# Row stores issued one at a time in the next block's gate steps, and a weight piece's bound and scale moved up by a step

## The chip, the cores and the metric

One core of one Trainium2 chip runs the whole program. The metric is the device time of one execution in microseconds (us). Three runs of the kernel before gave 1183.08 to 1185.95 us, with a median of 1185.08 us.

## The reference, cut to what matters

The program is an attention between tokens and states, a gated MLP and a mixture of experts with one expert per token, one after the other:

```
attention   B=8, H=8, S=512 tokens, 32 states, D=64:
            xread = softmax(x state^T) state;  sread = softmax(state x^T) x
            x = concat([xread, sread])  -> 8 * 544 = 4352 rows of 512
MLP         x = (sigmoid(x @ w_gate) * (x @ w_val)) @ w_out     512 -> 1536 -> 512
experts     logits = x @ g;  e = argmax(logits);  p = softmax(logits)[e]
            out[row] = p * (relu(x[row] @ w1[e]) @ w2[e])       8 experts, 512 -> 1024 -> 512
```

The MLP's weights come as 64-bit floats; the expert weights w1 and w2 as 32-bit floats.

## The kernel before, in words

Every large product is made of three 16-bit products: each operand is split into a high and a low half (`pair`, lines 313 to 322: ScalarE writes the high half, L321 or L318, and VectorE or GpSimd the low one, L322 or L319).

`token_block(b)` runs eight times, once for each of the B = 8 sequences. It has 12 gate steps (`gate_val`, one for each 128 columns of w_gate and w_val) and then 4 output steps (`mlp_out`, one for each 128 tokens). A gate step is 12 matmuls of 512 columns, six into each of two PSUM tiles (L682 to L684); there are four such tiles (`mm`), so TensorE can work on one gate step while the one before it is being read. Behind the matmuls stand, in this order, a sigmoid on ScalarE (L688, writes `g`), a product on VectorE (L690, `g` in place), a cast on ScalarE (L695, `acth`) and a subtraction on GpSimd (L696, `actl`). `g` has two buffers: the sigmoid of a gate step can't start before the subtraction of the gate step two back has read its buffer.

Between pieces of a block's own matmuls stand numbered slots. `mid()` counts them: two in each gate step (slots 1 to 24: one behind the gate's matmuls, one behind the subtraction) and three in each output step (slots 25 to 36). In a slot, `mid()` first runs the functions that were hung on that number with `at(slot, f)`: the next block's attention, the state's scale, and the routing. Then it takes one step (up to the next `yield`) of a background generator with `pump(bg)`, in the gate steps in two slots of three, in the output steps in each. In blocks 1 to 7 that generator is `conv_experts`: it converts 64 pieces (128x1024 elements) of the expert weights into high and low halves. Each piece takes three steps. Its parts: `load` (a transfer on SyncE's queue, L628), `bound` (ScalarE sums absolute values, L634, into `em`), `scale` (TensorE spreads `em` over the partitions, L202; VectorE takes the maximum, L209, and makes a power of two, L142 and L143, `inv`), `pair` with that scale (L321 and L322), and a store of the two halves to DRAM on GpSimd's queue (L667, `w_d`). The store of a piece is issued in the next piece's second step.

`route(q, ...)` makes the routing of block q's 512 tokens in four steps, in slots 27, 29, 34 and 36 of the same block (for q = 0 in slots 35 and 36 of block 0 and 3 and 6 of block 1). Its last step writes the weight and the number of each token into the row (L838, L839) and issues four indirect DMAs on GpSimd's queue (L842), one for each 128 rows, which put the rows where their expert will read them (`rows_d`). All write the same tensor, so each one waits for the landing of the one before it. `xrow` has four buffers, written again in the next block's output steps.

Behind the eight blocks, the 256 state rows take 12 gate steps of their own (with `hook(fc)` behind each), and then some 37 expert tiles follow, which read `rows_d` and the converted weights.

The order of TensorE's instructions is that of the program, written by hand. On the other engines a planner orders each engine's queue beforehand; each queue then runs strictly in order. In blocks 1 to 7, what a slot issues is pinned behind the last sigmoid and the last product issued so far (`behind`).

Of the kernel before, what the change touches and what calls it, by code (L numbers as in the profile page):

```python
# [26 lines left out]
def attention_moe_router_kernel(  # L27
# [25 lines left out]
    B, H, S, D = x.shape  # L53
# [79 lines left out]
    def tl(shape, dt=F32, name="t", bufs=None, pool=None):  # L133
        kw = {} if bufs is None else {"bufs": bufs}
        return (pool or tiny).tile(shape, dt, name=name, tag=name, **kw)
# [177 lines left out]
    def pair(v, h16, l16, s=None, inplace=False):  # L313

        if inplace:
            nc.scalar.activation(v, v, AF.Copy, scale=s)
        if s is None or inplace:
            nc.scalar.copy(h16, v)  # L318
            nc.gpsimd.tensor_tensor(l16, v, h16, op=ALU.subtract)  # L319
        else:  # L320
            nc.scalar.activation(h16, v, AF.Copy, scale=s)  # L321
            nc.vector.scalar_tensor_tensor(l16, v, s, h16, op0=ALU.mult, op1=ALU.subtract)  # L322
# [288 lines left out]
    def conv_experts():  # L611

        items = [(e, i, k) for e in range(NE) for i in range(NFQ) for k in range(2)]
        vs = {}
        sc = {}

        def load(n):
            if n >= len(items):
                return
            e, i, k = items[n]  # L620
            q = slice(i * FQ, (i + 1) * FQ)
            if k == 0:
                vs[n] = big_p.tile([P, NDC, FQ], F32, name="big", tag="big")
                src = w1[e, :, q].rearrange("(c p) f -> p c f", p=P)
            else:
                vs[n] = big_p.tile([P, FQ // P, DM], F32, name="big", tag="big")
                src = w2[e, q, :].rearrange("(g p) w -> p g w", p=P)
            nc.sync.dma_start(out=vs[n], in_=src)  # L628

        def bound(n):  # L630
            if n >= len(items):
                return
            sc[n] = tl([P, 1], name="em")
            nc.scalar.activation(junk8, vs[n].rearrange("p a f -> p (a f)"), AF.Abs,  # L634
                                 accum_out=sc[n], saturate=False)

        def scale(n):
            if n >= len(items):
                return
            e, i, k = items[n]  # L640
            sc[n], _ = pow2_scale(
                all_max(spread(sc[n]), "er"), 14, "es", inv=False,
                out=inv12[:, k, e, i:i + 1],
            )

        for n in range(3):
            load(n)
        yield
        yield
        bound(0)  # L650
        yield
        scale(0)
        yield
        late = None
        for n, (e, i, k) in enumerate(items):
            v = vs.pop(n)
            if k == 0:
                o = big_p.tile([P, NDC, 2, FQ], F16, name="out", tag="out", bufs=2)
                dst = w1_d[e, :, i]
            else:  # L660
                o = big_p.tile([P, FQ // P, 2, DM], F16, name="out", tag="out", bufs=2)
                dst = w2_d[e, :, 2 * i:2 * i + 2]
            pair(v, o[:, :, 0], o[:, :, 1], sc.pop(n))
            yield
            bound(n + 1)
            if late:
                nc.gpsimd.dma_start(out=late[0], in_=late[1])  # L667
            late = dst, o
            yield
            load(n + 3)  # L670
            scale(n + 1)
            yield
        nc.gpsimd.dma_start(out=late[0], in_=late[1])

# [81 lines left out]
    def route(q, n, acts):  # L756
# [3 lines left out]
        for a in range(NFC // 4):  # L760
            for l in range(2):
                for i in range(4):
                    fc = 4 * a + i
# [71 lines left out]
        for j in range(n):  # L835
# [11 lines left out]
                bounds_check=NROWS - 1,  # L847
                oob_is_err=False,
            )
        yield  # L850

    def counts(nm):

# [238 lines left out]
    UMAX = (((22, 23), (34, 36)), ((6, 8), (20, 22)), ((6, 8), (20, 22)))  # L1092
    EARLY = 34
    ROUTE = (27, 29, 34, 36)
    GV, ALL = 2 * NFC, 2 * NFC + 3 * NJ

    sr = {}
    gens = {}
    router = {}
# [16 lines left out]
    def token_block(b):  # L1116
        isig = states[b]["i"]
        acts = []
        sg = tl([P, NFC], name="sgf")
        todo = {}  # L1120

        def at(slot, f):
            todo.setdefault(slot, []).append(f)

        if b + 1 < B:
            if b == 0:
                for u, slots in ((state_max(1), (13, 15)), (unit_max(NU), (14, 16))):
                    for slot in slots:
                        at(slot, lambda u=u: next(u, None))
            at(2 if b else 19, lambda: state_turn(b + 1))  # L1130

            def first_step(n):
                gens[n] = att_unit(n)
                next(gens[n])

            for c in range(NU):
                n = NU * (b + 1) + c
                slots = (UNIT0, UNIT1)[b][c] if b < 2 else UNIT[c]
                if slots[0]:
                    at(slots[0], lambda n=n: first_step(n))  # L1140
                for slot in slots[1:]:
                    at(slot, lambda n=n: next(gens[n], None))
                if LOAD[min(b, 2)][c]:
                    at(LOAD[min(b, 2)][c], lambda n=n: unit_load(n + 1))
                um = unit_max(n + 1)
                for slot in UMAX[min(b, 2)][c]:
                    at(slot, lambda um=um: next(um, None))
            if 1 <= b < B - 2:
                at(EARLY, lambda: first_step(NU * (b + 2)))
                at(EARLY + 2, lambda: unit_load(NU * (b + 2) + 1))  # L1150
            for m in range(NFP):
                at(GV + 2 * m, lambda m=m: drain(deque([state_weights(b + 1, m)])))
        if b + 1 == B:
            rs = state_rows()
            at(6, lambda: next(rs, None))
            at(12, lambda: next(rs, None))
        if b + 2 < B:
            at(1 if b else 21, lambda: state_load(b + 2))
            sm = state_max(b + 2)
            at(9 if b else 30, lambda: next(sm, None))  # L1160
            at(12 if b else 33, lambda: next(sm, None))
        if b == 0:

            rw = router_weights()
            for slot in (25, 26, 27, 28, 29, 30, 31, 33):
                at(slot, lambda: next(rw, None))
        for slot in (35, 36) if b == 0 else ROUTE:
            at(slot, lambda: next(router[b], None))
        if b == 1:
            for slot in (3, 6):  # L1170
                at(slot, lambda: next(router[0], None))
        half = [0]

        def mid():
            half[0] += 1
            with behind() if b else ExitStack():
                for f in todo.get(half[0], ()):
                    f()
                if half[0] > 12 if b == 0 else half[0] > GV or half[0] % 3:
                    pump(bg)  # L1180

        if b > 0:
            nc.vector.tensor_scalar(
                sg, inv_w[:, 0], isig, 2.0 ** (M_SH - PR_SH), ALU.mult, ALU.mult
            )
        for fc in range(NFC):
            if b == 0 and fc % 2 == 0:
                fp = fc // 2
                if fp == 0:
                    ws = state_weights(0, 0)  # L1190
                    drain(deque([ws]))
                nc.vector.tensor_scalar(
                    sg[:, fc:fc + 2], inv_w[:, 0, fc:fc + 2], isig, 2.0 ** (M_SH - PR_SH),
                    ALU.mult, ALU.mult,
                )
                if fp + 2 < NFP:
                    cvs[fp + 2] = conv_wgv(fp + 2, raws.pop(fp + 2))
                    next(cvs[fp + 2])
                    if fp + 3 < NFP:
                        raws[fp + 3] = load_wgv(fp + 3)  # L1200
            elif b == 0 and fc // 2 + 2 < NFP:
                drain(deque([cvs.pop(fc // 2 + 2)]))
            gate_val(fc, S, sg, V_SH, token_chunks(b, fc), acts, mid)
            if b == 0 and fc + 2 < NFC:
                if fc % 2 == 0:
                    ws = state_weights(0, fc // 2 + 1)
                next(ws, None)
        if b == 0:
            drain(bg)
        rt_new(b, isig)  # L1210
        router[b] = route(b, NJ, acts)
        for j in range(NJ):
            mlp_out(NJ * b + j, j, acts, mid)
        if b == 0:
            bg.append(ce)
# [84 lines left out]
    n = B * NS  # L1300

    def hook(fc):

        if fc == 4:
            prelim()
            fetch_w(0, regs["e"], which=(0,))
        if fc == 8:
            fetch_w(0, regs["e"], which=(1,))
            for s in range(2):
                fetch_rows(s, regs["row"] + s * P)  # L1310
# [184 lines left out]
```

## Time and profile before

| what | value |
|---|---|
| runs of the kernel before | 1183.08, 1185.08, 1185.95 us |
| the profiled execution's own time | 1188.41 us |
| its span, first to last instruction | 1186.4 us |
| mean granted TensorE clock | 0.963 |
| busy in the span: TensorE matmuls, VectorE, ScalarE, GpSimd | 91%, 72%, 47%, 24% |
| indirect stores of rows (L842) | 34, mean 1162 ns of GpSimd each |
| pieces converted | 64 |

PE is TensorE, PEld its weight load, DVE VectorE, ACT ScalarE, POOL GpSimd, SP SyncE. "X <- Y" after an idle time says that the instruction waited for Y. The shares are averages over stages with different limits: blocks 1 to 7 lie between about 198 and 744 us, the state rows between 744 and 777 us, the expert tiles behind that.

### The profile page before, as it was taken

The page shows a single profiled execution, that of the slowest core. Times are in us where ns is not written, and L with a number is a line of the kernel's source. Part 1 is how long each engine was busy: PE and PEld are TensorE (multiplying, and loading weights), DVE is VectorE, ACT ScalarE, POOL GpSimd, SP SyncE. Part 2 cuts the span into 40 slices and gives each one's busy share as a digit, 9 for nine tenths or more (in the row PEclk, how much of TensorE's full clock was granted, in tenths as well). Part 3 has the DMA queues.
Part 4 walks back from the last instruction along what each step waited for, and adds up shares of the span by engine and source line. Part 5 has one row for each costly group of instructions (what it writes and reads, how often), then busy time and mean ns, then how long its engine had stood idle before and what let it go on. Part 6 is the DMA issues. An engine that isn't in the chain of part 4 may idle for free. (4 is left out here: it accounts for less than half of the span.)

```text
span 1186.4 us, 22619 instructions
## 1 busy us (share of the span) xinstructions
PE 1083.8 (91%) x8459; PEld 592.4 (50%) x8459; DVE 852.7 (72%) x2080; ACT 554.4 (47%) x967; POOL 284.8 (24%) x293
## 2 busy tenths in 40 slices
PE   3377489899899999998999999999999999999997
PEld 2222134344344444443444444856666667766675
DVE  7999775687888888978878765348666666665664
ACT  4666644676766858767668582311111111111111
POOL 1112200532524506324145171300100000000000
PEclk9678799999999999999999999999999999999999
DMA  7615492556647577466575452563321495979438
GB/s 257 199 56 160 107 173 57 154 145 192 203 134 222 166 179 228 142 170 201 137 232 152 143 205 77 156 223 128 74 55 39 116 364 116 319 255 379 71 81 298
DMA packets 187745, 200.66 MB, mean 169 GB/s; under 512 B 130159, under 2 KB 154735, under 8 KB 184304
## 3 DMA queue, kind: packets, MB, share of 16 engines
q1 hardware_dynamic: 172736, 147.51, 44.7%
q0 software_dynamic: 14896, 51.67, 11.5%
q8 instruction: 68, 1.11, 0.4%
q14 instruction: 45, 0.37, 0.1%
HBM read 217.40 MB, written 54.88 MB: 230 GB/s over the span
## 5 line engine op out<-in xcount | busy, mean ns | idle before, releaser
L930 ACT CAST acth<-v 128x256 f16<-128x256 f32 x148 | 59.9, 404 | 329.2 <-DVE v L929 299.1
L696 POOL TENSOR_TENSOR actl<-g,acth 128x512 f16<-128x512 f32 (+1 forms) x108 | 138.6, 1286 | 197.7 <-ACT acth L695 197.2
L684 PE MATMUL mm<-aT,M 128*128 128x512 f16 x384 | 152.5, 397 | 13.8 <-ACT M L510 13.8
L682 PE MATMUL mm<-aT,M 128*128 128x512 f16 x384 | 152.2, 396 | 14.0 <-ACT g L688 13.3
L739 PE MATMUL mm<-wout,acth 128*128 128x512 f16 x408 | 155.6, 381 | 9.5 <-DVE wout L607 8.5
L740 PE MATMUL mm<-wout,acth 128*128 128x512 f16 x408 | 155.4, 381 | 0.0
L741 PE MATMUL mm<-wout,actl 128*128 128x512 f16 x408 | 155.3, 381 | 0.0
L683 PE MATMUL mm<-aT,M 128*128 128x512 f16 x384 | 151.9, 395 | 0.0
L915 PEld LDWEIGHTS <-wgv 128*128 128x128 f16 x1184 | 115.8, 98 | 18.5 <-DMA wgv<-w_d 1.2
L915 PE MATMUL mm<-big,wgv 128*128 128x256 f16 x704 | 118.5, 273 | 0.7 <-DMA wgv<-w_d 0.7
L944 POOL DMA_INDIRECT out_dram<-g,meta x37 | 36.0, 972 | 344.4 <-DVE g L941 284.7
L918 PEld LDWEIGHTS <-wgv 128*128 128x128 f16 x1184 | 115.8, 98 | 4.0
L918 PE MATMUL mm<-big,wgv 128*128 128x128 f16 x704 | 117.3, 219 | 0.0
L928 DVE TENSOR_REDUCE v<-mm 128x256 f32<-128x512 f32 x148 | 101.4, 685 | 18.6 <-PE mm L918 18.6
L931 DVE TENSOR_TENSOR actl<-v,acth 128x256 f16<-128x256 f32 x148 | 62.8, 424 | 68.8 <-ACT acth L930 67.8
L322 DVE SCALAR_TENSOR_TENSOR out<-big,inv,out 128x1024 f16<-128x1024 f32 x64 | 82.9, 1295 | 36.3 <-ACT out L321 36.3
L690 DVE SCALAR_TENSOR_TENSOR g<-mm,g 128x512 f32<-128x512 f32 (+1 forms) x108 | 71.0, 657 | 50.7 <-PE mm L684 26.0
L321 ACT ACTIVATE out<-big,inv 128x1024 f16<-128x1024 f32 x64 | 73.2, 1144 | 52.6 <-DVE inv L143 45.5
L688 ACT ACTIVATE g<-mm,sgf 128x512 f32<-128x512 f32 (+1 forms) x108 | 71.4, 661 | 41.2 <-POOL actl L696 30.8
L695 ACT CAST acth<-g 128x512 f16<-128x512 f32 (+1 forms) x108 | 63.3, 588 | 41.2 <-DVE g L690 41.0
L667 POOL DMA_DIRECT2D w_d<-out x63 | 35.5, 563 | 189.3 <-DVE out L322 138.1
L915 PE MATMUL mm<-out,wgv 128*128 128x256 f16 x480 | 80.8, 273 | 0.0
(322 smaller groups left out, 2126.7 us busy)
## 6 DMA issues: line engine op xcount, KB each, us to landing
wgv<-w_d SPq DMA_DIRECT2D x56, 2048.0 KB
wout<-w_d SPq DMA_DIRECT2D x18, 2048.0 KB
big<-in_moe_w_dram SPq DMA_DIRECT2D x64, 512.0 KB
w_d<-out POOLq DMA_DIRECT2D x64, 512.0 KB, 5.1
xb<-in_x_dram SPq DMA_DIRECT2D x60, 128.0 KB
wgv<-in_moe_w_gate_dram SPq DMA_DIRECT2D x3, 1024.0 KB
wgv<-in_moe_w_val_dram SPq DMA_DIRECT2D x3, 1024.0 KB
wout<-in_moe_w_gate_dram SPq DMA_DIRECT2D x3, 1024.0 KB
```

The lines of the kernel that those rows point to most:

```text
L321: nc.scalar.activation(h16, v, AF.Copy, scale=s)
L322: nc.vector.scalar_tensor_tensor(l16, v, s, h16, op0=ALU.mult, op1=ALU.subtract)
L682: nc.tensor.matmul(ps[k], w[0], v[0], start=(i == 0), stop=False)
L683: nc.tensor.matmul(ps[k], w[0], v[1], start=False, stop=False)
L684: nc.tensor.matmul(ps[k], w[1], v[0], start=False, stop=(i == len(parts) - 1))
L696: last["P"] = nc.gpsimd.tensor_tensor(lo, g, h, op=ALU.subtract)
L739: nc.tensor.matmul(po, hj, wout[:, fc, 1], start=(fc == 0), stop=False)
L740: nc.tensor.matmul(po, hj, wout[:, fc, 0], start=False, stop=False)
L741: nc.tensor.matmul(po, lj, wout[:, fc, 1], start=False, stop=(fc == NFC - 1))
L915: nc.tensor.matmul(ph[:, i], w1s[:, pr, c, 0, f], t[:, :, c], start=(c == 0), stop=False)
L918: nc.tensor.matmul(ph[:, i, 1], w1s[:, pr, c, 1, f], t[:, 0, c], start=False, stop=(c == NDC - 1),)
L928: nc.vector.tensor_reduce(v, ph.rearrange("p i l q -> p i q l"), axis=AX.X, op=ALU.add)
```

## The change

The store of a row group ends a step of `route`, so its last step becomes four. The first of them stays in slot 36 (block 0: slot 6 of block 1); the other three go to slots 3, 7 and 11 of the next block (10, 14 and 18 in block 1), and for the last block to the first three `hook` calls of the state rows. Only the two copies into the row and the indirect DMA of a group move; the arithmetic ahead of them stays in the first of the four steps.

In `conv_experts`, `bound(n + 1)` is issued ahead of `pair` of piece n in its first step, no longer in its second; `scale(n + 1)` in the second step, no longer in the third. `load(n + 3)` and the store stay where they were, and a piece still has three steps.

```
 conv_experts:
+            bound(n + 1)
             pair(v, o[:, :, 0], o[:, :, 1], sc.pop(n))
             yield
-            bound(n + 1)
+            scale(n + 1)
             if late:
                 nc.gpsimd.dma_start(out=late[0], in_=late[1])
             late = dst, o
             yield
             load(n + 3)
-            scale(n + 1)
             yield
 route, behind the indirect DMA of row group j:
                 oob_is_err=False,
             )
-        yield
+            yield
 constants:
     ROUTE = (27, 29, 34, 36)
+    ROWS = ((10, 14, 18), (3, 7, 11))
 token_block(b):
+        if b > 0:
+            for slot in ROWS[b > 1]:
+                at(slot, lambda: next(router[b - 1], None))
 hook(fc):
+        if fc < 3:
+            next(router[B - 1], None)
```

## Rows read from the trace of the kernel before

**Rows 1.** Blocks 1, 2, 4, state rows: PE PEld DVE ACT POOL busy, PEclk.
```profile
198.00:286.00 88.00, 80.46 (x576) 35.56 (x575) 67.86 (x200) 58.24 (x95) 28.30 (x27) 0.96 0.52 146
286.00:369.00 83.00, 79.54 (x582) 35.34 (x581) 67.87 (x175) 58.85 (x95) 29.14 (x29) 0.98 0.61 181
...
445.00:521.00 76.00, 74.01 (x556) 33.31 (x553) 64.74 (x160) 53.26 (x89) 29.68 (x28) 1.00 0.62 178
744.00:777.00 33.00, 33.00 (x287) 27.79 (x285) 8.79 (x40) 10.65 (x25) 12.79 (x18) 1.00 0.59 199
```

**Rows 2.** Waits of TensorE between 198 and 720 us: total, times, longest.
```profile
PE mm L682 <- ACT g L688: 9.4, 5, 3.4
PE at L202 <- ACT junk L634: 4.6, 5, 1.4
PE at L807 <- DVE roh L800: 2.3, 1, 2.3
```

**Rows 3.** Waits of the other engines in the same stretch.
```profile
ACT g L688 <- POOL actl L696: 30.8, 21, 3.9
POOL rows_d L842 <- DMA rows_d<-xrow,rri: 28.6, 15, 3.6
```

**Rows 4.** Timeline of block 1: start, duration, engine and line, idle before.
```profile
228.70 1.03 POOL L842 DMA_INDIRECT rows_d<-xrow,rri  x1 [2.99 <-DMA rows_d<-xrow,rri]
229.73 1.19 POOL L696 TENSOR_TENSOR actl<-g,acth 128x512 f16<-128x512 f32 x1
...
230.96 0.69 ACT L688 ACTIVATE g<-mm,sgf 128x512 f32<-128x512 f32 x1 [3.91 <-POOL actl L696]
...
231.69 0.38 PE L682 MATMUL mm<-aT,M 128*128 128x512 f16 x1 [3.44 <-ACT g L688]
...
231.91 0.38 PE L683 MATMUL mm<-aT,M 128*128 128x512 f16 x1
```

**Rows 5.** Behind a wait of block 1, of block 2; columns as above.
```profile
231.70:235.50 3.80, 3.80 (x11) 1.36 (x11) 1.80 (x5) 3.05 (x6) 2.23 (x2) 0.56 0.33 138
307.20:310.60 3.40, 3.40 (x9) 1.21 (x8) 3.40 (x7) 1.01 (x2) 0.74 (x2) 0.51 0.27 78
```

**Rows 6.** Timeline of block 2 around 303 us.
```profile
303.52 0.99 POOL L842 DMA_INDIRECT rows_d<-xrow,rri  x1 [3.60 <-DMA rows_d<-xrow,rri]
...
303.78 4.66 DVE L337 SCALAR_TENSOR_TENSOR xn<-xb,uxs,xn 128x256 f16<-128x256 f32 x4 [1.55 <-issue]
...
305.09 2.27 POOL L696 TENSOR_TENSOR actl<-g,acth 128x512 f16<-128x512 f32 x2
...
307.03 0.41 PE L682 MATMUL mm<-aT,M 128*128 128x512 f16 x1 [2.06 <-ACT g L688]
```

**Rows 7.** The four instructions of line 337 in that stretch: min/median/max ns.
```profile
L337 DVE SCALAR_TENSOR_TENSOR xn<-xb,uxs,xn x4: 472/478/3471, 303.8 to 308.0; 128x256 f16<-128x256 f32 x4
```

**Rows 8.** Line 842 in the whole span: min/median/max on GpSimd, and to landing.
```profile
L842 POOL DMA_INDIRECT rows_d<-xrow,rri x34: 974/1021/2232, 212.5 to 801.6; - x34
...
DMA to landing us min/median/max: 2.8/3.6/6.7
```

**Rows 9.** Groups of instructions by line: busy us, mean ns, idle before.
```profile
L321 ACT ACTIVATE out<-big,inv 128x1024 f16<-128x1024 f32 x64 | 73.2, 1144 | 52.6 <-DVE inv L143 45.5 <-DVE cum L817 7.0
...
L634 ACT ACTIVATE junk<-big 128x1024 fp8e5<-128x1024 f32 x64 | 67.3, 1052 | 0.0
...
L634 ACT ACTIVATION_READ_ACCUMULATOR junk<-big 128x1 f32 x64 | 12.5, 196 | 0.0
```

**Rows 10.** Timeline of block 2: a spread that waits for its bound.
```profile
314.17 0.23 PE L202 MATMUL at<-identb,em 128*128 128x128 bf16 x1 [1.40 <-ACT junk L634]
```

**Rows 11.** ScalarE in block 6: a sigmoid that waits.
```profile
620.83 0.69 ACT L688 ACTIVATE g<-mm,sgf 128x512 f32<-128x512 f32 x1 [3.53 <-POOL actl L696]
```

**Rows 12.** Busy time in a stretch of block 6 and one of block 3.
```profile
620.00:630.00 10.00, 10.00 (x51) 4.21 (x49) 4.60 (x9) 8.31 (x14) 5.48 (x6) 1.00 0.62 173
370.00:400.00 30.00, 28.84 (x154) 12.95 (x153) 22.89 (x62) 24.54 (x41) 18.74 (x17) 1.00 0.73 236
```

More of the change, by code (lines that the diff above doesn't have):

```diff
@@ L662, in conv_experts @@
                 dst = w2_d[e, :, 2 * i:2 * i + 2]
+            bound(n + 1)
             pair(v, o[:, :, 0], o[:, :, 1], sc.pop(n))
             yield
-            bound(n + 1)
+            scale(n + 1)
             if late:
@@ L670, in conv_experts @@
             load(n + 3)
-            scale(n + 1)
             yield
@@ L849, in route @@
             )
-        yield
+            yield
     def counts(nm):
@@ L1094, in attention_moe_router_kernel @@
     ROUTE = (27, 29, 34, 36)
+    ROWS = ((10, 14, 18), (3, 7, 11))
     GV, ALL = 2 * NFC, 2 * NFC + 3 * NJ
@@ L1171, in token_block @@
                 at(slot, lambda: next(router[0], None))
+        if b > 0:
+            for slot in ROWS[b > 1]:
+                at(slot, lambda: next(router[b - 1], None))
         half = [0]
@@ L1302, in hook @@
     def hook(fc):
+        if fc < 3:
+            next(router[B - 1], None)
         if fc == 4:
```

## Prediction, made before the result was known

> **What bounds the kernel now.** I read the busy time by stretch first. From the blocks on, TensorE's matmuls fill nearly all of the time: the state rows are full to the last tenth, block 4 has 74 us of work in 76 us, and so have blocks 3, 6 and 7 or nearly. Blocks 1 and 2, and 5, which repeats 2, stand out, with 88 and 83 us and a granted clock under 1.00 [rows 1]. So time can be won only where TensorE waits or runs slowly, and the waits are few. Between 198 and 720 us they are: 9.4 us in five waits for a sigmoid (L682 <- L688), 4.6 us in five waits of the spread for a bound (L202 <- L634), and 2.3 us for the routing in block 1 [rows 2]; all others are under 1.3 us in sum.
>
> Next I asked what the sigmoid waited for. On ScalarE it stood 30.8 us, 21 times, for the subtraction that frees a `g` buffer, and GpSimd, whose subtraction it is, stood 28.6 us, 15 times, in a row store that waits for the landing of the one before [rows 3]. The timeline of block 1 shows one such chain whole: the store waits 2.99 us, the subtraction queued behind it starts at 229.73 us, the sigmoid at 230.96, the matmul at 231.69 after 3.44 us of idling [rows 4]. In the 3.8 us behind it the granted clock was 0.56 of the full level, nearly all of it at 1.2 in place of 2.4 GHz; behind the like wait of block 2 it was 0.51 over 3.4 us, and the same in block 5 [rows 5]. A wait for a store thus costs its own length and then half of some 3.5 us.
>
> Blocks 2 and 5 have one link more. There the fourth store waited 3.60 us; then two subtractions ran back to back for 2.27 us, and TensorE idled for 2.06 us [rows 6]; block 5 has the same chain. Beside them, one of four equal VectorE instructions took 3471 ns, where the median is 478 [rows 7].
>
> **The change part by part.**
>
> *The stores.* No store is taken away: 34 before and after, 1.02 us of GpSimd each, 3.6 us to landing, 6.7 at most [rows 8]. What moves is when each is queued. Before, all four are issued in one slot, and the planner lays them between the subtractions of the first gate steps, where the next one comes up before the last has landed. After, they come four slots apart. A gate step is 12 matmuls, 0.22 us apart [rows 4], so 2.6 us, and four slots are two of them, 5.2 us. A store and its landing take 1.0 + 3.6 = 4.6 us: the median one no longer waits. The longest (1.0 + 6.7 = 7.7 us) still would, for 2.5 us. Behind a store on GpSimd stand the subtraction and then a piece's store to DRAM; for the subtraction waits the sigmoid two gate steps on, and for that the matmuls.
>
> What this frees: the five waits, 9.4 us [rows 2], and the slow stretches behind three of them. From the clock rows: 3.8 x (1 - 0.56) + 2 x 3.4 x (1 - 0.51) = 1.7 + 3.3 = 5.0 us [rows 5]. Bounds: nothing, if another wait takes their place, and 14.4 us. I take all of it here, and put what comes back into a term of its own.
>
> *The two copies into the row* move with each store; they are single elements on VectorE, which is busy for 22.89 of 30 us in the gate steps [rows 12]. Nothing is added to their number; I take 0.
>
> *The last block's stores* come one gate step of the state rows apart: 33 us for 12 steps, 2.75 us [rows 1], under the 4.6 us that a store needs, so they go on waiting, by some 1.9 us each. TensorE is busy for 33.00 of 33.00 us there now [rows 1], with the same four stores in the same stretch; that work hides them. Without this cover it would be 3 x 1.9 = 5.7 us. I take 0. The first read of the rows is issued five gate steps behind the last store, 13.7 us, which is more than the longest landing.
>
> *Bound and scale.* A bound is 1052 + 196 ns of ScalarE, the high half 1144 ns [rows 9]. Before, they stood in two steps, high half first; after, both in the first step, bound first. The spread keeps its distance of one step from the bound. Where that is one slot, 1.3 us, it is about the bound's own length, and TensorE waits whenever ScalarE is behind: in block 2 the spread at 314.17 us came after 1.40 us of it [rows 10]. Gain: the bound no longer stands behind a high half that itself waits for the scale (45.5 us of waiting before L321 [rows 9], most of it in output steps, where it costs nothing). Bounds: all 4.6 us of the spread's waits [rows 2] on one side; on the other, as much again, because the rotation of three steps over the slots is the same and the waits may only move. Nearest is the row of block 2, where ScalarE had just come out of the store's backlog: I take 1 us of gain. The load has to be there a step earlier; before, no bound ever waited (idle 0.0 [rows 9]), so I take 0, and at most one output slot of 2.6 us at a time.
>
> *What comes back.* In the gate steps ScalarE is busy for 24.54 of 30 us [rows 12]; with GpSimd free, it is the next to be late. Bound and high half in one slot are 2.4 us of it, where before at most 1.25 us came at once. A sigmoid of block 6, however, started 3.53 us late [rows 11], and TensorE was busy for 10.00 of the 10.00 us around it [rows 12]. So a delay of this size by itself is taken up by the four PSUM tiles; only delays that meet reach TensorE. Bounds: 0, and 1.25 us for each of the 37 pieces that fall into gate steps (64 x 16 of 28 steps), 46 us. Near the lower end: I take 3 us for this and for stores that still wait.
>
> *Sum.* -9.4 - 5.0 - 1 + 3 = -12.4 us. The profiled execution took 1188.4 us, so 1176.0; it stands 3.3 us above the median of the runs, which makes **1173 us**.
>
> **The rivals.**
>
> *Half of it.* In blocks 2 and 5 the late part is also VectorE's: 3471 against 478 ns is 3.0 us [rows 7], and it ends with the two subtractions, not with the store. If those two waits come about without the stores, only 9.4 - 2 x 2.06 = 5.3 us and one slow stretch of 1.7 us go, less the 2 us that come back on balance: -5 us, **1180 us**. For it: the change removes no subtraction. Against it: they were back to back because a store had held them. The Trainium skill ("SBUF — State Buffer", Who interferes with whom) has a rule on this side: a VectorE instruction with two SBUF inputs and a GpSimd instruction that reads SBUF exclude each other, for the whole instruction. By that rule these meetings stay possible wherever the stores stand, and the time would be that of this rival; the long instruction of line 337 fits it.
>
> *More.* The spread's waits go too and little comes back: -9.4 - 5.0 - 4.6 + 1 = -18 us, **1167 us**. For it: the longest of the five, 1.40 us, is the one just behind the backlog of block 2 [rows 10], and block 5 has its like. Against it: the other three stand elsewhere.
>
> *No change that can be told.* ScalarE is the next limit at once, and each sigmoid is late behind a bound and a high half where it was late behind a store: the five waits shrink by a third, 3 us, the slow stretches stay, and 1 us comes back: **1183 us**. For it: 24.54 of 30 us [rows 12]. Against it: the 3.53 us that cost nothing [rows 11, 12].
>
> *Slower.* The pair of 2.4 us in one slot ahead of a sigmoid. If 0.6 us of it reached TensorE for each of 37 pieces, that is 22 us against 14.4 won: +8 us, **1193 us**. It decides from 14.4 / 37 = 0.39 us for each piece. For it: ScalarE's 82% in such a stretch [rows 12]. Against it: a longer delay of one sigmoid, 3.53 us, was taken up whole [rows 11, 12].
>
> **How the numbers follow.** Forecast 0.58 (its own range 1168 to 1178), half 0.11, more 0.09, no change 0.13, slower 0.09. A measurement of this kernel can tell about 0.3% (3.6 us) from no change: the first three are faster, 0.78; same 0.13; slower 0.09. The range goes down just past the case of more, 1165, and up to 1183, past the half and to the time of no change, which leaves out some 0.18: the slower case, half of no change, and the tail under 1165.
>
> **What would show it.** Right: GpSimd's waits of line 842 for a landing fall from 28.6 us to under 10, ScalarE's waits for GpSimd from 30.8 to under 15; TensorE's five waits for the sigmoid are gone or under 2 us in sum; blocks 2 and 5 last some 77 us at a clock of 1.00; block 1 keeps the 2.3 us for the routing. Wrong: the stores no longer wait, and TensorE still idles at L682 (no change), or waits at L202 and L682 appear that are short, many, and spread over all blocks (slower); or line 337 still has an instruction of 3 us in blocks 2 and 5 (half).

## The result, and the profile after

The changed kernel took 1193.57 us (median of 6 runs, 1191.26 to 1197.49) beside 1185.51 us for the kernel before (6 runs, 1183.08 to 1186.8). The ratio is 1.0068, 95% interval [1.0042, 1.0094]: 8 us slower, where 12 us of gain were forecast. The profiled execution of the changed kernel took 1192.08 us, 3.7 more than that of the kernel before; it lies 1.5 us under its median, as the one of before lies 3.3 above.

The page's first part, then the instructions of line 842 with their landing:

```profile
span 1190.4 us, 22630 instructions
...
PE 1079.2 (91%) x8459; PEld 592.3 (50%) x8459; DVE 856.9 (72%) x2080; ACT 554.5 (47%) x967; POOL 275.4 (23%) x293
```

```profile
L842 POOL DMA_INDIRECT rows_d<-xrow,rri x34: 978/1019/1432, 210.1 to 805.7; - x34
...
  DMA rows_d<-xrow,rri: 5.1, 4
...
DMA to landing us min/median/max: 2.8/3.5/5.1
```

The stores did what was expected. In the blocks they hardly wait for each other's landing any more: 28.6 us in 15 waits before, between 198 and 720 us [rows 3], and 1.4 us in one wait after. The other three of the four waits shown (3.8 us) lie in the state rows. The waits of TensorE between 198 and 720 us, then one of ScalarE (total, times, longest), show what that was worth:

```profile
PE at L365 <- DMA xT<-xn: 16.6, 5, 8.1
PE at L202 <- ACT junk L634: 3.5, 3, 1.9
PE at L807 <- DVE roh L800: 2.3, 1, 2.3
...
PE mm L682 <- ACT g L688: 0.3, 1, 0.3
```

```profile
ACT g L688 <- POOL actl L696: 21.9, 22, 2.6
```

The wait for the sigmoid fell from 9.4 to 0.3 us [rows 2]. A wait that was no row of the argument took its place: 16.6 us at L365, the scores of the next sequence's attention, for `xT`, which SyncE's transposing DMA (L344) makes out of `xn`. Before, it was 0.5 us.

By blocks (distance from the first gate matmul of one block to that of the next, from the timeline), blocks 1 to 7 took 86.5, 80.3, 77.2, 77.5, 80.2, 75.5 and 66.2 us before, and 85.0, 78.7, 78.2, 87.3, 77.0, 76.3 and 66.2 after. Blocks 1, 2 and 5 won 6.3 us; block 4, where nothing was to be won, lost 9.8. The state rows took 48.2 us both times. Blocks 1, 2, 4 and part of the state rows in the columns of [rows 1] (DMA share and GB/s at the end):

```profile
198.00:283.00 85.00, 77.09 (x568) 34.06 (x567) 67.17 (x198) 60.04 (x96) 27.27 (x27) 0.98 0.60 159
283.00:361.70 78.70, 76.67 (x562) 34.24 (x561) 64.57 (x169) 54.67 (x91) 27.86 (x28) 0.98 0.61 177
439.90:527.20 87.30, 77.36 (x563) 34.23 (x562) 65.27 (x172) 57.12 (x94) 27.90 (x28) 0.94 0.62 168
...
748.00:781.00 33.00, 33.00 (x290) 28.06 (x288) 9.30 (x41) 11.24 (x25) 12.76 (x18) 1.00 0.58 191
```

Block 4 now has 77.36 us of TensorE in 87.3 us, at a clock of 0.94. Before, the same block was nearly full, at 1.00:

```profile
442.10:519.60 77.50, 75.51 (x568) 33.96 (x565) 66.24 (x169) 54.63 (x90) 29.68 (x28) 1.00 0.63 180
```

The place in block 4 where the time is lost, after, from four engines' queues (an SPq row starts when the DMA is issued; line 333 makes the high half of `xn`; a piece's store is line 667 before and 668 after):

```profile
457.45 1.14 ACT L333 ACTIVATE xn<-xb,uxs 128x1024 f16<-128x1024 f32 x1
462.56 1.78 SPq L285 DMA_DIRECT2D xb<-in_x_dram  x4
464.38 3.40 SPq L344 DMA_TRANSPOSE xT<-xn  x1
464.85 0.59 POOL L668 DMA_DIRECT2D w_d<-out  x1 [3.43 <-DVE sgs L143]
467.88 2.28 SPq L628 DMA_DIRECT2D big<-in_moe_w_dram  x2
474.85 1.49 PE L365 MATMUL at<-xT,bdT 128*64 128x512 f16 x6 [8.13 <-DMA xT<-xn]
```

and the same place before:

```profile
456.11 1.15 ACT L333 ACTIVATE xn<-xb,uxs 128x1024 f16<-128x1024 f32 x1
462.35 1.78 SPq L285 DMA_DIRECT2D xb<-in_x_dram  x4
464.17 2.98 SPq L344 DMA_TRANSPOSE xT<-xn  x1
465.96 0.58 POOL L667 DMA_DIRECT2D w_d<-out  x1
467.25 9.91 SPq L628 DMA_DIRECT2D big<-in_moe_w_dram  x3
469.88 0.84 PE L365 MATMUL at<-xT,bdT 128*64 128x512 f16 x6 [0.48 <-DMA xT<-xn]
```

The transpose is issued at nearly the same time, 464.2 and 464.4 us, with the same four x loads just ahead of it and a piece's load 3.1 and 3.5 us behind it. Before, its reader started 5.7 us later; after, 10.5 us later. A piece's store of 512 KB came 1.79 us behind the transpose before, and 0.47 us after. Measured from the block's first gate matmul (442.1 us before, 439.2 after), TensorE was ready for L365 at the same point, 27.3 and 27.5 us; but the transpose was issued 22.1 us into the block before and 25.2 after, since the high half of `xn` began at 14.0 and 18.2 us. So to the 0.5 us of before, two parts were added: 3 us of a later issue and 4.8 us of a slower transfer. Two-microsecond windows over the stretch (columns as above) show the DMA engines in it, after:

```profile
466.00:468.00 2.00, 0.72 (x4) 0.10 (x2) 1.97 (x5) 1.44 (x2) 1.85 (x2) 1.00 1.23 129
468.00:470.00 2.00, 0.00 (x0) 0.00 (x0) 1.93 (x4) 2.00 (x4) 0.67 (x1) 0.85 1.42 126
470.00:472.00 2.00, 0.00 (x0) 0.00 (x0) 0.35 (x1) 0.42 (x2) 0.57 (x1) 0.50 1.19 113
...
476.30:479.80 3.50, 3.50 (x11) 1.25 (x10) 0.68 (x2) 2.14 (x4) 0.00 (x0) 0.52 0.39 156
```

and before:

```profile
466.00:468.00 2.00, 2.00 (x11) 0.94 (x10) 1.97 (x7) 1.71 (x3) 1.54 (x3) 1.00 1.25 227
468.00:470.00 2.00, 1.52 (x9) 0.55 (x9) 0.98 (x2) 2.00 (x5) 0.15 (x1) 1.00 0.87 248
```

They are at least as busy as before and move half as much: 113 to 129 GB/s, not 227 to 248. The last row of after is the second price of an idle TensorE: 3.5 us at a clock of 0.52 behind the wait. The Trainium skill ("DMA: Bandwidth & Descriptors", Issuing engines are not separate DMA queues) says that transfers issued from different engines run on the same 16 DMA engines and interleave. The trace fits that: the transpose stands on SyncE's queue and the store on GpSimd's, and the one took 10.5 us with the other close behind. Whether the one slows the other is put to the test below (store_short).

### The profile page after: what moved, and what is told of

The parts are those of the page before. It is cut to its first block, busy times and chain, and to the rows that moved or that the text cites. A ratio compares the mean times of both kernels' runs of the same rounds, so it can differ in the third digit from the quotient of the medians.

```text
span 1190.4 us, 22630 instructions
## 1 busy us (share of the span) xinstructions
PE 1079.2 (91%) x8459; PEld 592.3 (50%) x8459; DVE 856.9 (72%) x2080; ACT 554.5 (47%) x967; POOL 275.4 (23%) x293
## 5 line engine op out<-in xcount | busy, mean ns | idle before, releaser
L696 POOL TENSOR_TENSOR actl<-g,acth 128x512 f16<-128x512 f32 (+1 forms) x108 | 133.8, 1243 | 189.3 <-ACT acth L695 187.5
L739 PE MATMUL mm<-wout,acth 128*128 128x512 f16 x408 | 155.6, 381 | 8.9 <-DVE wout L607 8.9
L682 PE MATMUL mm<-aT,M 128*128 128x512 f16 x384 | 151.4, 394 | 6.8 <-ACT g L688 5.0
L322 DVE SCALAR_TENSOR_TENSOR out<-big,inv,out 128x1024 f16<-128x1024 f32 x64 | 88.7, 1386 | 26.7 <-ACT out L321 26.2
L688 ACT ACTIVATE g<-mm,sgf 128x512 f32<-128x512 f32 (+1 forms) x108 | 71.0, 660 | 37.9 <-POOL actl L696 21.9
L498 ACT ACTIVATE M<-mm 128x512 f16<-128x512 f32 x96 | 52.1, 593 | 72.3 <-PE mm L489 72.2
```

What stands on the lines that cost most here:

```text
L682: nc.tensor.matmul(ps[k], w[0], v[0], start=(i == 0), stop=False)
L696: last["P"] = nc.gpsimd.tensor_tensor(lo, g, h, op=ALU.subtract)
L739: nc.tensor.matmul(po, hj, wout[:, fc, 1], start=(fc == 0), stop=False)
```

## The experiments

Times are medians; each ratio is to the kernel before in the same series, with its 95% interval. The last columns are TensorE's waits between 198 and 720 us in each profile, in us: all of the list added up, and of these the waits for `xT` (L365), of the spread for a piece's bound (L202 <- L634), and for the sigmoid (L682 <- L688; 0 where the list has none).

| kernel | us | ratio | all | xT | bound | sigmoid |
|---|---|---|---|---|---|---|
| before | 1185.51 to 1187.52 | 1 | 19.7 | 0.5 | 4.6 | 9.4 |
| after | 1193.57 | 1.0068 [1.0042, 1.0094] | 26.6 | 16.6 | 3.5 | 0.3 |
| after_again | 1191.94 | 1.0048 [1.0029, 1.0066] | 24.9 | 13.0 | 4.3 | 0.3 |
| stores_only | 1187.21 | 0.9998 [0.9977, 1.0018] | 20.7 | 1.2 | 8.1 | 1.6 |
| conv_only | 1189.81 | 1.0029 [1.0007, 1.0052] | 22.6 | 6.1 | 7.4 | 0 |
| load_behind | 1184.81 | 0.9997 [0.9976, 1.0019] | 20.7 | 0.6 | 6.7 | 0.9 |
| scores_later | 1186.91 | 1.0010 [0.9990, 1.0031] | 20.1 | 5.1 | 5.9 | 1.9 |
| store_third | 1196.80 | 1.0098 [1.0073, 1.0123] | 28.6 | 16.3 | 3.4 | 0.8 |
| store_short | 1189.13 | 1.0025 [1.0003, 1.0047] | 21.0 | 8.4 | 3.6 | 0.5 |
| before_load_behind | 1183.57 | 0.9994 [0.9977, 1.0012] | 18.0 | 0 | 6.3 | 2.7 |
| stores_load_behind | 1190.05 | 1.0022 [1.0003, 1.0040] | 22.3 | 0 | 6.4 | 2.0 |
| bound_alone | 1182.05 | 0.9964 [0.9949, 0.9979] | 15.8 | 0 | 0 | 0.9 |
| bound_alone_old_stores | 1184.66 | 0.9978 [0.9957, 0.9999] | 17.1 | 0 | 0 | 3.4 |
| umax_later | 1180.08 | 0.9943 [0.9921, 0.9965] | 16.9 | 0 | 0 | 2.4 |
| umax_later_again | 1180.30 | 0.9949 [0.9930, 0.9968] | 16.8 | 0 | 0 | 2.3 |
| umax_later_old_stores | 1186.50 | 1.0012 [0.9993, 1.0031] | 21.2 | 0 | 0 | 3.6 |
| before_umax_later | 1186.54 | 1.0003 [0.9981, 1.0024] | 19.6 | 0 | 10.3 | 2.4 |
| after_umax_later | 1184.05 | 0.9985 [0.9968, 1.0001] | 19.4 | 0.6 | 6.1 | 0.6 |

The waits are those of one execution each, the times medians of six or more; where a kernel was profiled twice, the sums are 26.6 and 24.9, and 16.9 and 16.8 us. Two things are read from the table at once. The ratio goes with the sum of the waits, not with any one of them: over 24 us the kernel is slower by about 0.5% or more, under 17.5 faster, and from 18.0 to 22.6 no ratio is more than 0.3% from 1. And the sigmoid's 9.4 us shrink in every other kernel, in those too that leave the row stores where they were (0 in conv_only, 2.7 in before_load_behind, 2.4 in before_umax_later), while the sums of these three are 22.6, 18.0 and 19.6. In before_load_behind GpSimd still waits 26.3 us for the landings of row stores. So those five waits hang on more than the stores: on how the other work of the slots is laid around them.

### Each half of the change alone

stores_only has the moved row stores, and `bound` and `scale` where they were. conv_only has the reverse.

> The kernel after with bound and scale back in their old steps, so only the row stores are moved. Theory A (with the stores out of the way TensorE reaches the scores' matmuls, L365, before the transposing DMA of xn has landed): the waits of L682 for a sigmoid stay under 2 us in sum, those of L365 for the DMA are 5 us or more, time 1183 to 1191 us. Theory B (the moved bound and scale bring the loads and stores of the pieces on top of the transpose): L365 waits under 3 us in sum, time 1172 to 1178 us.

> The kernel before with bound and scale moved alone; the row stores stay four in a slot. Theory A: L682 still waits 8 us or more for sigmoids, L365 under 3 us for the DMA, time 1182 to 1188 us. Theory B: L365 waits 8 us or more although the stores have not moved, time 1190 us or more.

TensorE's waits of stores_only:

```profile
PE at L202 <- ACT junk L634: 8.1, 8, 1.8
PE at L384 <- DVE uxr L209: 4.7, 2, 2.3
...
PE mm L682 <- ACT g L688: 1.6, 5, 0.6
PE at L365 <- DMA xT<-xn: 1.2, 1, 1.2
```

and of conv_only:

```profile
PE at L202 <- ACT junk L634: 7.4, 5, 2.3
PE at L365 <- DMA xT<-xn: 6.1, 3, 4.0
```

The moved stores alone free the sigmoid and hardly make `xT` late; what they free goes to L202 and L384, and the time is that of before. The moved bound and scale alone free the sigmoid as well, with the stores in their old place, bring the first 6.1 us for `xT`, and cost 0.3%. The 16.6 us need both halves; no theory had that right.

### Is it the transpose?

load_behind issues the second unit's transpose ahead of the next sequence's x loads on SyncE's queue. Against after:

```
-    LOAD = ((19, 24), (3, 12), (0, 12))
+    LOAD = ((19, 24), (3, 14), (0, 14))
```

scores_later gives the same transpose two slots more until its reader, in blocks 1 to 6 (UNIT1 has the same edit):

```
-    UNIT = ((0, 2, 8, 13, 24, 27, 28, 33), (9, 13, 19, 23, 25, 30, 32, 36))
+    UNIT = ((0, 2, 8, 13, 24, 27, 28, 33), (9, 13, 21, 24, 25, 30, 32, 36))
```

> The kernel after with the load of the next unit's x (four DMAs, L285) hung on slot 14 in place of 12, behind the transpose (slot 13) on SyncE's queue. If the transpose is late because it stands behind these four issues (1.8 to 2.1 us), it is issued that much sooner, the waits at L365 fall from 16.6 us to about 9, and the time to about 1186 us. If it is late because other transfers slow it down while it runs, the waits stay within 3 us of 16.6 and the time within 3 us of the kernel after.

> The kernel after with the second unit's scores (L365) in slot 21 in place of 19 and its next product (L384) in 24 in place of 23, so that the transpose has two slots, 2.6 us, more. Theory A: the five waits at L365 of 3.7, 2.0, 1.7, 8.1 and 1.2 us fall to about 1.1, 0, 0, 5.5 and 0, in sum from 16.6 to 6.6 us, and the time by about 10 us to 1183 us. Rival: the wait passes on to L384, one slot closer now, and the time stays within 3 us of the kernel after.

The timeline of load_behind in block 4:

```profile
459.46 1.69 SPq L344 DMA_TRANSPOSE xT<-xn  x1
461.20 3.52 SPq L285 DMA_DIRECT2D xb<-in_x_dram  x4
...
461.75 0.59 POOL L668 DMA_DIRECT2D w_d<-out  x1 [3.42 <-DVE sgs L143]
...
464.24 0.84 PE L365 MATMUL at<-xT,bdT 128*64 128x512 f16 x6 [0.61 <-DMA xT<-xn]
```

4.8 us from issue to use in place of 10.5, the waits for `xT` down from 16.6 to 0.6 us, and the ratio from 1.0068 to 0.9997. The first theory had the direction but only a part of it, about 9 us of waits left: the transpose was not only issued sooner (1.8 us, measured from the moment at which TensorE is ready for it), it also landed 5.7 us faster, now with the x loads behind it and the piece's store 2.3 us behind it. scores_later, which moves only the reader, says the same: 5.1 us are left (0.9 in block 1, 4.2 in block 4), and the ratio is 1.0010; the waits fell as its theory A has it, but the time only to that of before, not to 1183 us. Either edit takes the loss against before away, so that loss is the late transpose. But the time only came back to that of before. In load_behind the bound's spread waited 6.7 us, and L384 4.3 us for a tile that the maximum of the attention scale (`uxr`, L209) still held.

### What makes the transpose late?

after_again is the changed kernel once more. store_third puts the piece's store into the third step:

```
             scale(n + 1)
+            yield
             if late:
                 nc.gpsimd.dma_start(out=late[0], in_=late[1])
             late = dst, o
-            yield
             load(n + 3)
```

store_short leaves out three quarters of the store of two pieces, those that meet the transposes of blocks 1 and 4 (not shown: block 0 fills their other rows with zeros):

```
 +    SHORT = (1, 29)
...
-                nc.gpsimd.dma_start(out=late[0], in_=late[1])
+                if n - 1 in SHORT:
+                    nc.gpsimd.dma_start(out=late[0][0:32], in_=late[1][0:32])
+                else:
+                    nc.gpsimd.dma_start(out=late[0], in_=late[1])
```

> The kernel after, unchanged, a second time beside the others. If the late transposes are a property of its order, L365 waits 14 to 19 us again, with 7 to 9 us of it in block 4, and the time is 1191 to 1196 us. If the 8.1 us of block 4 were an accident of the one execution, the sum of the waits at L365 is under 10 us.

> The kernel after with the store of a piece's halves (w_d, L668) in the third step in place of the second; the row stores, bound, scale and x loads as in the kernel after. Theory (the transposes of blocks 1 and 4 take 10 to 11 us from issue because the piece's store is issued on top of them): they land 5 to 7 us after their issue, the waits at L365 fall from 16.6 us to 8 or less, time 1184 to 1188 us. Rival (the four loads of x ahead of them on the same queue are what slows them): latency stays at 9 us or more in block 1 or 4, waits 13 us or more, time 1190 us or more.

> The kernel after, but the stores of the two pieces that go out 0.5 us behind the transposes of blocks 1 and 4 (pieces 1 and 29) carry a quarter of their bytes: 32 of 128 partitions; the other rows of these two pieces are filled with zeros in block 0, so the output is not the reference's there. Theory (the piece's store on top of the transpose is what makes it land 10 to 11 us after its issue): it lands within 7 us in blocks 1 and 4, L365 waits 6 us or less where the kernel after had 16.6 and 13.0, time 1183 to 1188 us. Rival (the four x loads ahead of it are enough): it lands after 9 us or more, the waits and the time stay within 2 us of the kernel after.

The wait is no chance: 13.0 us again, 7.8 of it in block 4. store_third tells nothing of the cause, since the store didn't move in time: it comes behind its low half on VectorE, and still stood 0.5 us behind the transposes of blocks 1 and 4. (It is slower still, 1.0098, for a reason that was not looked for.) store_short, in block 4 (its lines are numbered one or two higher):

```profile
459.47 3.68 SPq L345 DMA_TRANSPOSE xT<-xn  x1
459.93 0.56 POOL L670 DMA_DIRECT2D w_d<-out  x1 [3.42 <-DVE sgs L144]
467.53 1.49 PE L366 MATMUL at<-xT,bdT 128*64 128x512 f16 x6 [5.72 <-DMA xT<-xn]
```

With a quarter of the bytes behind it, the transpose took 8.1 us in place of 10.5. In block 1 its reader started 7.3 us after the issue without any wait, where after had 11.0 us and a wait of 3.66. The time (1.0025) lies between before and after, with an interval that meets that of after, so it is the waits that tell here and not the time.

The other profiles settle what 8.1 us means. After's own block 2 has the same four x loads ahead of the transpose, and no store within 3 us behind it:

```profile
305.50 3.61 SPq L344 DMA_TRANSPOSE xT<-xn  x1
308.61 0.57 POOL L668 DMA_DIRECT2D w_d<-out  x1
311.51 0.84 PE L365 MATMUL at<-xT,bdT 128*64 128x512 f16 x6 [1.97 <-DMA xT<-xn]
```

That one took 6.0 us. In all the profiles together, a whole store was issued 0.4 to 0.5 us behind the second unit's transpose nine times (after, after_again, scores_later and store_third in blocks 1 and 4, conv_only in block 1): it took 10.1 to 11.9 us each time. The others for which TensorE waited, with no store that close, took 4.6 to 8.1 us, and all but two of them (load_behind, after_umax_later) had the four x loads ahead. So the close store makes the step to over 10 us, and the x loads alone do not; with a quarter of the store, the transpose is back among the others. What spreads these from 4.6 to 8.1 us was not separated. Of after's 16.6 us, 11.8 lie in the two blocks with the close store; the other 4.8 us, in blocks 2, 3 and 5, came because TensorE was ready for L365 sooner in the block (27.2, 26.9 and 27.9 us into it, before 32.3, 28.0 and 32.2).

### What takes the freed time once the transpose is in time?

bound_alone is load_behind with `scale` back in the third step, so that only the bound is moved; bound_alone_old_stores has the four row stores in one slot as well. before_load_behind and stores_load_behind add the later x loads to before and to stores_only.

```
 conv_experts, bound_alone against after:
             yield
-            scale(n + 1)
             if late:
...
             load(n + 3)
+            scale(n + 1)
             yield
```

> The kernel after with the x loads in slot 14 (as in load_behind) and the scale back in its old third step, so that a spread comes two steps behind its bound. Theory A2 (what kept load_behind at the time of before is the distance of one step between bound and spread): L202 waits under 2 us for bounds where load_behind had 6.7, TensorE idles 16 us or less between 190 and 830 us where it had 20.9, time 1178 to 1182 us. Rival (the gate steps have no slack on ScalarE and VectorE, so each wait removed comes back at another line): L202's waits fall and others rise, 19 to 22 us in sum, time 1183 to 1188 us.

> The kernel before with only the x loads moved to slot 14. If the order of the x loads matters only once the stores no longer hold TensorE up, the time is within 2.5 us of the kernel before and L365's 0.5 us of waits goes to 0. If it is an independent gain, the time is 1182 us or less.

> As bound_alone (bound first, scale in the third step, x loads in slot 14), but with the four row stores back in one slot. If moving the row stores is worth something once the transposes are in time and the spread has its distance, this is slower than bound_alone by 3 us or more (1185 us or more) and L682 waits 4 us or more for sigmoids. If the gate steps give back whatever is taken, it is within 2 us of bound_alone.

> Only the row stores moved, and the x loads in slot 14; bound and scale as in the kernel before. If the bound ahead of the high half is what made bound_alone faster than before, this is back at 1184 us or more with 5 us or more of waits at L202 for bounds. If the row stores did it, it is at 1182 us or less like bound_alone.

With two steps between bound and spread, L202's waits for L634 are gone and the ratio is 0.9964, about what theory A2 has. Two of its largest waits left are for the maximum of the attention scale (`uxr`, L209):

```profile
PE at L202 <- DVE uxr L209: 4.5, 2, 2.4
...
PE at L384 <- DVE uxr L209: 1.8, 2, 0.9
```

The x loads do not do that alone: they bring nothing to before (0.9994), and together with the moved row stores, but with the old order of bound and high half, they leave 6.4 us at L202 and 1.0022. Whether the row stores count was not told apart here: 0.9964 with them moved and 0.9978 with them in one slot, with intervals that overlap.

### The version that beats both, and what it needs

umax_later is bound_alone with the spread of the attention scale two slots later. Three others take a part out of it: umax_later_old_stores the moved row stores, before_umax_later all of the change (only the two lines of slots stay), after_umax_later the third-step scale.

```
-    UMAX = (((22, 23), (34, 36)), ((6, 8), (20, 22)), ((6, 8), (20, 22)))
+    UMAX = (((22, 23), (34, 36)), ((6, 8), (20, 24)), ((6, 8), (20, 24)))
```

> bound_alone with the second unit's spread of its x maximum in slot 24 in place of 22, behind the product L384 (slot 23). bound_alone idled 6.3 us for tiles that VectorE's maximum of that spread (uxr, L209) still held. If these waits are real room, they go and the time falls by 4 us or more to 1178 us or less. If VectorE is the limit there, the idle time of TensorE stays within 2 us of bound_alone's 16.4, at other lines, and so does the time.

> The best version once more, beside the three others. Theory A (the gain is in the distance between a bound or a maximum and its spread): 0.994 of the kernel before, as measured. Theory B (that was chance): 0.997, the value of bound_alone.

> The best version with the four row stores back in one slot. Theory A (the freed sigmoid waits are worth their 9.4 us once nothing else takes them): the five waits of L682 for a sigmoid come back, 3 to 9 us on TensorE, and the ratio is 0.998 to 1.002, at least 0.4% above umax_later_again. Theory B (gate steps give back elsewhere what one wait frees): within 0.2% of umax_later_again.

> The kernel before with the loads of the next sequence in slot 14 and the spread of the second attention scale in slot 24; nothing of the change. Theory A (the two parts of the change that stay are needed): 0.998 to 1.000, the five sigmoid waits as before. Theory B (the slots alone make the gain): 0.994 to 0.996.

> The whole change, with a piece's scale in its second step, and the two slots. Theory A (the distance from bound to spread matters as much as the two slots): L202 waits 5 us or more for the bounds of L634, and the ratio is 0.997 to 1.000. Theory B (only the two slots matter): L202 under 2 us, 0.993 to 0.995.

0.9943 and 0.9949 in two series: 6 to 7 us faster than before, 12 to 15 faster than after by the ratios. What the later spread adds to bound_alone (0.9964) is not told from nothing, since the intervals overlap: the 6.3 us of waits for `uxr` are gone, but the sum of the waits is 16.9 us where bound_alone had 15.8. TensorE's waits in umax_later_again:

```profile
PE mm L489 <- DVE M L500: 5.1, 7, 1.6
PE at L202 <- DVE er L209: 3.0, 2, 1.6
...
PE mm L682 <- ACT g L688: 2.3, 2, 1.1
PE mm L739 <- ACT g L688: 2.1, 4, 1.2
```

and, with the row stores back in one slot (umax_later_old_stores), TensorE's and then GpSimd's:

```profile
PE mm L739 <- ACT g L688: 3.9, 3, 1.6
PE mm L682 <- ACT g L688: 3.6, 3, 1.6
...
PE at L202 <- ACT xT L404: 3.4, 1, 3.4
```

```profile
POOL rows_d L842 <- DMA rows_d<-xrow,rri: 15.7, 12, 3.1
```

Here the row stores do count: without their move the whole gain is gone, 1186.5 against 1180.3 us, with intervals that don't meet. The sigmoid (both lines) waits 7.5 us in place of 4.4. Blocks 1 to 7 take 540.4 us in place of 533.6 in the two profiles, which fits the 6.2 us; the list of waits names 4.4 of it (21.2 less 16.8 us). The longest single one is the 3.4 us in block 4, for a ScalarE step of the attention (L404), so the 6.2 us are what the move of the stores is worth there, not what the sigmoid alone waits. The slots without the change bring nothing (1.0003; its sigmoid waits did not stay as before, as expected, but fell to 2.4 us, with 10.3 at L202), and the change with the slots but with its short distance from bound to spread gets 0.9985, with 6.1 us of waiting at L202.

## Why the prediction was wrong

*The step that failed* is the one that ends "I take all of it here, and put what comes back into a term of its own", with that term, "3 us for this and for stores that still wait". The five waits did go (9.4 to 0.3 us), and so did the slow stretches behind three of them. But a wait that the list puts down to the sigmoid is the last of several that came nearly together, and what stood close behind had no term. Of those the sum looked at ScalarE's burst alone; it left out the transposing DMA, whose reader is hung six slots behind it. The row was there: 0.5 us at L365 in one wait, among those "under 1.3 us in sum" (each of them; together they are 3.4 us). That transfer came just in time before. After the change TensorE was ready for L365 sooner in blocks 1, 2, 3 and 5, in block 4 the transpose was issued 3 us later in the block, and in blocks 1 and 4 a piece's store was issued 0.5 us behind it. In place of the 3 us, 16.3 us of waits came back: 26.6 in the list, of which before had 10.3 besides the sigmoid's. Three stretches at half the clock behind the waits for `xT` (233.7 to 237.5, 312.3 to 315.9, 476.3 to 479.8 us, at 0.55, 0.53 and 0.52) cost another 5.1 us, as much as those that went. By these lists the balance is 7 us of loss, between the 3.7 us of the two profiled executions and the 8.1 us of the medians. That `xT` makes the loss is shown by load_behind and scores_later; that a freed wait turns into others, by stores_only, and by conv_only, in which the sigmoid's waits go without any store being moved, and the kernel is slower. Why the planner put the high half of `xn` 4.2 us later into block 4 was not tested; on VectorE, the scale that it needs (`uxs`, L143) stood directly behind a maximum (L377) in the kernel before; in the kernel after, a product and two copies into a row stand between them.

Point by point:

- *Stores*: right. The median one waits no more for a landing in the blocks. The working counts a store's 1.0 us on GpSimd twice, since the 3.6 us to landing run from the store's start: where a store waits for a landing in the state rows, the starts are 3.1 us apart. The 12 gate steps of the state rows, too, took 31.5 us and not 33 (from the first gate matmul, at 741.5 us, to the first matmul of L739). With these values the verdict is the same. In the state rows three waits of at most 1.4 us were left, as before (1.9 each expected), under a TensorE that was busy for 33.00 of 33.00 us. The first read of the rows was issued 4.4 us behind the last of these stores, not 13.7, before as after.
- *ScalarE's waits for GpSimd*: 30.8 to 21.9 us, where under 15 was expected. The rest is mostly not the row stores': the subtraction waited for stood directly behind one in 11 of 21 waits before (22.4 us), and in 5 of 22 after (4.5 us).
- *The slow stretches*: expected gone. Three stand behind the waits for `xT` instead. Of the blocks 2 and 5, only 5 came to the expected 77 us at 1.00; 2 took 78.7 us at 0.98.
- *Bound and scale*: 1 us of gain expected; conv_only measured 3.4 us of loss (0.29% of 1186.9). The distance of one step between bound and spread stayed, as the prediction said, and that distance was the point: with two steps (bound_alone) L202's waits for the bound vanish.
- *What comes back*: the mechanism named, ScalarE's burst of bound and high half, shows at most in L202's waits (3.5 us), not at L682 (0.3 us for the sigmoid).
- *The rivals*: the time was that of "slower" (1193), by coincidence, for the mechanism was not: its short waits of many pieces at L202 and L682 did not come; five long waits for one DMA did. "No change" would have been right of stores_only, with L202 and L384 where it named the sigmoid. "Half" did not come either: line 337's longest instruction fell from 3471 [rows 7] to 1776 ns, and blocks 2 and 5 won 4.8 us. The Trainium skill's rule ("SBUF — State Buffer", Who interferes with whom: a VectorE instruction with two SBUF inputs contends with a GpSimd instruction that reads SBUF) did not give the time of this rival. No run here tests whether it has a part in the late transpose: the four instructions of line 337 ahead of it in block 4, 1.66 us long elsewhere, took 4.5 us from start to end before and 3.9 us after.

The stores' gain could be had all the same, once the next waits had been given distance: 6.2 us between umax_later_again and umax_later_old_stores, about half of the 12.4 forecast. Why it is 0.6% there, and not told from nothing in bound_alone against bound_alone_old_stores (0.9964 and 0.9978), stays open; the spread of the attention scale, which bound those two alike (4.5 and 5.1 us at L202), may have covered it.

## What to carry to other kernels

When a stall on the bounding engine is removed, list every other producer that this engine meets in the same stretch, DMAs above all, with its issue, its landing and its reader: here a wait of 0.5 us in the list was a transfer without slack, not a harmless one. Go by the sum of its waits, not by the one that goes: here each half of the change and the moved slots were worth nothing or less alone, and the right set of them 6 us. It is worth issuing a transfer with a deadline ahead of the others on its queue (here the waits for it fell from 16.6 to 0.6 us), and looking at its distance to a large store on another queue.

## What was not expected of the hardware

The same transposing DMA took 4.8 us from issue to its reader's start (load_behind), 5.7 (before) and 10.5 to 11.9 us (after, store_third) in block 4. TensorE waited for it in each, so this is the time to its landing. A store of 512 KB on another engine's queue, issued 0.5 us behind it, stands in each of the slow cases; with a quarter of that store's bytes the transfer took 8.1 us. In the slow case the DMA engines' busy share was 1.2 to 1.4, and they moved 113 to 129 GB/s; the share alone does not tell it from the stretch of before, with 1.25 at 227 GB/s. The store beside it took 9.8 us to land in after, and 5.1 us in before.
